# Gated attention and gated FFN on one core: which engine waits for the landings of all transfers at the program's end

## The chip, the cores and the metric

The kernel runs on one core of a Trainium2 chip. The core has five engines with a program each: TensorE (PE in the profile; PEld are its weight loads), VectorE (DVE), ScalarE (ACT), GpSimd (POOL) and SyncE (SP). They meet only through semaphores. Transfers between the chip's memory and the core are issued from an engine's queue and raise a semaphore when they land. The metric is the device time of one execution in microseconds (us); several executions are timed and the median is given.

## The reference

Two branches work on 2048 tokens of width 512, and a gate mixes them. Branch A is a linear-memory attention with 32 heads of width 16 in 4 segments of 512 tokens; branch B is a gated FFN of width 1792. Both read the same x.

```python
g = sigmoid((x * gate_w).sum(-1, keepdims=True))
a = A(x)                                   # attention with memory, then @ wo
b = ((relu(x @ W_gate)) * (x @ W_up)) @ W_down
out = g * a + (1 - g) * b

# A, for each segment s of 512 tokens (q, k, v = x @ wq, x @ wk, x @ wv):
p = softmax(q_s @ k_s.T / 4 + causal_mask)
a_mem = (phi(q_s) @ M) / (phi(q_s) @ z + 1e-6)     # phi(t) = t + 1 if t > 0 else exp(t)
o_s = sigmoid(beta) * a_mem + (1 - sigmoid(beta)) * (p @ v_s)
M, z = M + phi(k_s).T @ v_s, z + phi(k_s).sum()
```

The output is 2048 x 512 in bf16.

## The kernel before

The work is cut into 4 segments of 512 tokens, as the reference has them. For each segment there are projections (q, k, v), attention tiles of scores that ScalarE turns into exponentials and GpSimd masks, products with v, the memory's update and reading, the FFN in 14 slices of 128 columns, and at the end of a segment's work the output product. `outp` (L1056 and after) forms the output of 128 tokens at a time: the products with `wo` (L1074) and with `wd` (L1081) are summed in one PSUM bank, VectorE (L1090) or ScalarE (L1091) scales the bank into a buffer `osb`, and SP issues the store to `out` (L1093). The last tile of 128 tokens is split in columns 0 to 384 and 384 to 512, each with its own scaling and its own store; the store of the last 128 columns, 32 KB, is the last transfer of the program.

The order of all this is not written by hand. `program` describes each operation with its engine or engines, a planned duration and what it reads and writes; a list scheduler (`Sched`) places the operations one after the other on the engines by planned start times, and keeps for every engine a list `prog[engine]` of waits and instructions. `Sched.place` spreads the transfers over 16 semaphores, `dma0` to `dma15`. It takes the one whose last transfer is planned to land first, and has the issuing engine wait for that earlier transfer. `sc.semval` is the value that a semaphore has after a transfer, `sc.cnt` counts the transfers on it, and `sc.dma_end` is the planned landing of its latest one. Almost all transfers are issued from SP's queue; ScalarE issues three small ones at the start.

`Sched.emit` then writes the lists out, engine by engine: an item `("wait", semaphore, value)` becomes a `wait_ge` (L534), and any other item the instruction itself. A wait stands in its engine's program in order: what follows it on that engine starts after it.

After the scheduler has run, the last lines of `program` append waits for the latest transfer of each of the 16 semaphores, in the order of their planned landings, the latest first, so that the program doesn't end before the last transfer has landed. This list is appended to SP's program. Nothing is put on any engine's list behind it.

```python
    sc.run()
    for i in sorted(range(sc.ndma), key=lambda i: -sc.dma_end.get(i, 0.0)):
        if sc.cnt[f"dma{i}"]:
            sc.prog["sp"].append(("wait", f"dma{i}", sc.semval[f"dma{i}", sc.cnt[f"dma{i}"]]))
```

Of the kernel before, what the change touches and what calls it, by code (L numbers as in the profile page):

```python
# [560 lines left out]
def build_kernel(nc, A_x, A_wq, A_wk, A_wv, A_wo, A_beta, W_g, W_u, W_d, gate_w, out):  # L561
    _, S, D = A_x.shape
    F = W_g.shape[1]
    assert D == 512 and S % 512 == 0 and F % 128 == 0
    NSEG, KT, NF, NT = S // 512, D // 128, F // 128, S // 128
    EPS, SCALE = 1e-6, 16 ** -0.5
    sc = Sched(seeds=(237719, 74891, 0, 89398, 0, 53401, 416309, 0, 0, 0, 710933, 0, 718714, 120896, 538430, 820480, 585027, 870794, 793690, 0, 589972, 0, 0, 0, 454998, 16783, 0,))
    T = {}
    with contextlib.ExitStack() as stack:
        for name, shape, dt in plan(S, D, F):  # L570
            T[name] = stack.enter_context(nc.sbuf_tensor(name, shape, dt))
        PS = stack.enter_context(nc.psum_tensor("ps", [128, 8, 512], F32))
        for st in sc.streams:
            sc.sem[st] = stack.enter_context(nc.semaphore(f"s_{st}"))
        program(sc, nc, T, PS, A_x, A_wq, A_wk, A_wv, A_wo, A_beta, W_g, W_u, W_d, gate_w, out, NSEG, KT, NF, NT, EPS, SCALE)
        sc.emit(nc)
    return sc


def program(sc, nc, T, PS, A_x, A_wq, A_wk, A_wv, A_wo, A_beta, W_g, W_u, W_d, gate_w, out, NSEG, KT, NF, NT, EPS, SCALE):  # L580
# [583 lines left out]
    sc.run()  # L1164
    for i in sorted(range(sc.ndma), key=lambda i: -sc.dma_end.get(i, 0.0)):
        if sc.cnt[f"dma{i}"]:
            sc.prog["sp"].append(("wait", f"dma{i}", sc.semval[f"dma{i}", sc.cnt[f"dma{i}"]]))


def bass_gated_mix__memory_aug_infini_attn__glu_gated_reglu__prompt_kernel(  # L1170
# [31 lines left out]
```

## Time and profile before

| what | value |
|---|---|
| median of 3 runs | 263.29 us (262.95 to 263.42) |
| profiled execution's own time | 263.54 us |
| its span, first to last instruction of the program | 262.3 us |
| granted TensorE clock | 1.000 |
| TensorE busy | 255.7 us, 97% of the span |
| ScalarE, VectorE, GpSimd busy | 184.5, 179.5, 130.7 us |
| moved by transfers | 19.87 MB |

The profile is of one execution. Its span goes from the first to the last instruction of the program; the execution's own time is 1.24 us longer than the span. A row of a timeline gives the start in us from the span's start, the length in us, the engine, the line of the kernel, the operation with its tiles, and in brackets how long the engine sat idle before and what ended that. SPq and ACTq are instructions of an engine's sequencer, such as waits and issues of transfers; they are not counted as busy time. An EVENT_SEMAPHORE is a wait that stands as an instruction of its own. The list of issues gives for a transfer the time from its issue to its landing.

### The profile page before, as it was taken

How to read it: one execution, taken by the hardware profiler on the slowest of the kernel's cores; microseconds unless marked ns; L12 is line 12 of the kernel's file. 1: busy time of each engine (PE TensorE's matmuls, PEld its weight loads, DVE VectorE, ACT ScalarE, POOL GpSimd, SP SyncE). 2: the span in 40 equal slices, each digit the busy share in tenths (PEclk: the TensorE clock that was granted, in tenths of full speed). 3: DMA queues.
4: the chain of work that ended last, by engine and by line, in shares of the span. 5: the costliest groups of instructions: out<-in, count | busy, mean ns of one | idle time of the engine just before them, and what ended most of it. 6: DMA issues, size and time to landing. Idle time of an engine off the chain costs nothing.

```text
span 262.3 us, 6420 instructions
## 1 busy us (share of the span) xinstructions
PE 255.7 (97%) x2619; PEld 114.7 (44%) x2653; DVE 179.5 (68%) x356; ACT 184.5 (70%) x160; POOL 130.7 (50%) x295
## 2 busy tenths in 40 slices
PE   8999999999999999999999999999999999999997
PEld 5444443444344544434444544444444444444444
DVE  5488878788986577778788577757667716467600
ACT  4586689999789779785778687677777665576021
POOL 3036557564646457666645457846364454545100
PEclk9999999999999999999999999999999999999999
DMA  6999746930261135212040232010132100100011
GB/s 200 290 308 249 162 63 135 287 46 22 66 143 40 24 74 109 62 23 24 19 107 7 56 96 27 2 41 2 22 82 43 23 21 22 40 2 2 0 42 40
DMA packets 34925, 19.87 MB, mean 76 GB/s; under 512 B 24016, under 2 KB 34128, under 8 KB 34896
## 3 DMA queue, kind: packets, MB, share of 16 engines
q1 hardware_dynamic: 34800, 19.46, 31.6%
q8 instruction: 21, 0.34, 0.6%
q14 instruction: 8, 0.07, 0.1%
q10 hardware_dynamic: 96, 0.00, 0.0%
HBM read 10.40 MB, written 2.11 MB: 48 GB/s over the span
## 4 chain that ended last, share of the span: by engine, by line
PE 97%; issue 1%; DVE 1%
PE ps L1042 38%; PE ps L1081 19%; PE ps L792 11%; PE ps L912 9%; PE ps L968 6%; PE ps L790 5%; PE ps L1074 5%; PE ps L855 1%; PE ps L692 1%; PE ps L706 1%; PE ps L835 0%; DVE hT L1053 0%; DVE Tn L978 0%; DVE osb L745 0%; DVE osb L1090 0%
## 5 line engine op out<-in xcount | busy, mean ns | idle before, releaser
L934 POOL TENSOR_SCALAR_AFFINE_SELECT E<-E 64x256 bf16<-64x256 bf16 (+1 forms) x256 | 110.3, 442 | 112.2 <-ACT E L928 82.9
L928 ACT ACTIVATE E<-ps 128x2048 bf16<-128x2048 f32 x72 | 135.1, 1876 | 38.7 <-PE ps L912 38.6
L1042 PE MATMUL ps<-xT,wu 128*128 128x512 bf16 x213 | 57.2, 380 | 1.4 <-issue 1.3
L1042 PE MATMUL ps<-xT,wg 128*128 128x512 bf16 x219 | 57.7, 380 | 0.6 <-issue 0.3
L1081 PE MATMUL ps<-wd,hT 128*128 128x512 bf16 (+2 forms) x229 | 52.8, 367 | 0.9 <-issue 0.6
L1053 DVE TENSOR_TENSOR hT<-ps,rl 128x512 bf16<-128x512 f32 x56 | 38.5, 687 | 16.6 <-PE ps L1042 16.4
L1081 PEld LDWEIGHTS ps<-wd,hT 128*128 128x128 bf16 x238 | 21.4, 98 | 23.8 <-issue 2.4
L1042 PEld LDWEIGHTS ps<-xT,wg 128*128 128x128 bf16 x224 | 20.6, 98 | 25.7 <-issue 2.8
L1042 PEld LDWEIGHTS ps<-xT,wu 128*128 128x128 bf16 x224 | 20.1, 98 | 25.4 <-issue 3.5
L912 PE MATMUL ps<-qT,kp 32*128 32x192 bf16 (+7 forms) x512 | 28.6, 287 | 0.0
L978 DVE STREAM_TRANSPOSE Tn<-ps 128x512 f32<-128x512 f32 x32 | 21.3, 696 | 8.7 <-PE ps L968 8.7
L1051 DVE TENSOR_SCALAR rl<-ps 128x512 bf16<-128x512 f32 x30 | 20.7, 690 | 8.5 <-PE ps L1042 8.2
L1090 DVE TENSOR_SCALAR osb<-ps,omg 128x512 bf16<-128x512 f32 (+1 forms) x8 | 5.6, 701 | 26.0 <-PE ps L1081 15.1
L1050 ACT ACTIVATE rl<-ps 128x512 bf16<-128x512 f32 x26 | 15.5, 598 | 10.0 <-PE ps L1042 9.7
L912 PEld LDWEIGHTS ps<-qT,kp 32*128 32x128 bf16 x512 | 8.2, 92 | 25.3 <-issue 13.1
L968 PE MATMUL ps<-E,vaug 64*17 64x128 bf16 (+7 forms) x512 | 18.7, 283 | 0.0
L968 PE MATMUL ps<-E,vsh 64*17 64x128 bf16 (+7 forms) x512 | 18.3, 283 | 0.0
L1091 ACT ACTIVATE osb<-ps,omg 128x512 bf16<-128x512 f32 (+1 forms) x9 | 6.1, 674 | 16.4 <-PE ps L1074 14.0
L792 PE MATMUL ps<-xT,wq 128*128 128x512 bf16 x61 | 16.0, 390 | 0.4 <-issue 0.3
L1074 PE MATMUL ps<-wo,oT 128*128 128x512 bf16 (+2 forms) x67 | 16.2, 366 | 0.2 <-issue 0.2
L792 PE MATMUL ps<-xT,wk 128*128 128x512 bf16 x60 | 15.6, 380 | 0.4 <-issue 0.3
L968 PEld LDWEIGHTS ps<-E,vaug 64*17 64x17 bf16 x512 | 11.6, 86 | 8.5 <-issue 4.4
(68 smaller groups left out, 233.6 us busy)
## 6 DMA issues: line engine op xcount, KB each, us to landing
vsh<-vaug SPq DMA_DIRECT2D x8, 272.0 KB, 4.2
osb<-in_A_x_dram SPq DMA_DIRECT2D x16, 128.0 KB, 2.3
out_dram<-osb SPq DMA_DIRECT2D x15, 128.0 KB, 1.7
wg<-in_B_W_gate_dram SPq DMA_DIRECT2D x8, 224.0 KB, 5.7
wu<-in_B_W_up_dram SPq DMA_DIRECT2D x8, 224.0 KB, 6.2
wd<-in_B_W_down_dram SPq DMA_DIRECT2D x1, 1792.0 KB, 10.6
hT<-in_A_x_dram SPq DMA_DIRECT2D x2, 256.0 KB, 2.9
wq<-in_A_wq_dram SPq DMA_DIRECT2D x4, 128.0 KB, 3.5
```

What stands on the lines that cost most here:

```text
L792: ins = e.matmul(A(ep)[:, :], lhsT=w[:, kt, col * 128:(col + 1) * 128], rhs=V.xT[:, kt, tok:tok + 512], start=(kt == 0), stop=(kt == KT - 1))
L912: ins = q.matmul(dst, lhsT=V.kp[r, kslot(s, G), c, :], rhs=V.qT[r, qslot(s, G), q0:q0 + w], start=True, stop=True, tile_position=(32 * jj, ...
L928: acts.append(act(lambda a: a.activation(V.E[:, base * 512:base * 512 + min(2048, 4 * W)], PF[:, 0:min(2048, 4 * W)], ACT.Exp, scale=SCALE ...
L934: pools.append(pool(lambda g, ap=ap, lim=lim, pat=pat: g.affine_select(out=ap, in_=ap, compare_op=ALU.is_ge, fill=0.0, base=lim, pattern=[ ...
L968: ins = q.matmul(A(eps[p])[32 * jj:32 * jj + 17, 64 * (c + u):64 * (c + u + n)], lhsT=v[:, 8 * G + 2 * jj + p, :], rhs=V.E[r, f:f + 64 * n ...
L978: ds.append(dve(lambda e, p=p, ep=eps[p]: e.transpose(V.Tn[:, 2 * (G % (TNN // 2)) + p, :], A(ep)[:, :]), t_dve(512), writes=[f"Tn{2 * (G ...
L1042: ins = e.matmul(A(ep)[:, :], lhsT=w[:, kt, f * 128:(f + 1) * 128], rhs=V.xT[:, kt, c % XR * 512:(c % XR + 1) * 512], start=(kt == 0), sto ...
L1050: evs.append(sc.add(Op([("act", lambda e, ep=eg, r=r: e.activation(V.rl[:, r, :], A(ep)[:, :], ACT.Relu), t_act(512)), ("dve", lambda e, e ...
L1051: ("dve", lambda e, ep=eg, r=r: e.tensor_scalar(V.rl[:, r, :], A(ep)[:, :], 0.0, None, ALU.max), t_dve(512))],
L1053: evs.append(dve(lambda e, ep=eu, r=r, hs=hs: e.tensor_tensor(V.hT[:, hs, :], A(ep)[:, :], V.rl[:, r, :], ALU.mult), t_dve(512), reads=[f" ...
L1074: ins = e.matmul(A(ep)[:, 0:c1 - c0], lhsT=V.oT[:, ot[G], i * 128:(i + 1) * 128], rhs=V.wo[:, G, c0:c1], start=st_ and G == 0, stop=sp_ an ...
L1081: ins = e.matmul(A(ep)[:, 0:c1 - c0], lhsT=V.hT[:, slots[f], i * 128:(i + 1) * 128], rhs=V.wd[:, f, c0:c1], start=st_ and f == f0, stop=sp ...
```

## The change

The 16 waits are appended to ScalarE's program in place of SP's. The list, its order and its values are the same, and so is all that the scheduler placed before it: the loop runs after `sc.run()`. ScalarE's last instruction ahead of the waits is then its last scaling at L1091, and SP's last instruction is the issue of the last store at L1093.

```diff
--- before.py
+++ after.py
@@ -1164,7 +1164,7 @@
     sc.run()
     for i in sorted(range(sc.ndma), key=lambda i: -sc.dma_end.get(i, 0.0)):
         if sc.cnt[f"dma{i}"]:
-            sc.prog["sp"].append(("wait", f"dma{i}", sc.semval[f"dma{i}", sc.cnt[f"dma{i}"]]))
+            sc.prog["act"].append(("wait", f"dma{i}", sc.semval[f"dma{i}", sc.cnt[f"dma{i}"]]))
```

## The prediction

> **What bounds the kernel now.** I read the page first, for the shares and the chain that ended last.
>
> ```profile
> span 262.3 us, 6420 instructions
> PE 255.7 (97%) x2619; PEld 114.7 (44%) x2653; DVE 179.5 (68%) x356; ACT 184.5 (70%) x160; POOL 130.7 (50%) x295
> ...
> PE 97%; issue 1%; DVE 1%
> ```
>
> TensorE is busy 255.7 of 262.3 us, and the chain of work that ended last is 97% matmuls. The edit touches none of that: it is about what happens after the last matmul. So the second view is the end of the timeline, ScalarE, VectorE and the issues of SP's queue together.
>
> ```profile
> 256.52 0.69 ACT L1091 ACTIVATE osb<-ps,omg 128x512 bf16<-128x512 f32 x1 [3.20 <-PE ps L1074]
> ...
> 259.44 0.58 ACT L1091 ACTIVATE osb<-ps,omg 128x384 bf16<-128x384 f32 x1 [2.24 <-PE ps L1074]
> 259.97 0.27 PEld L1074 LDWEIGHTS ps<-wo,oT 128*128 128x128 bf16 x4
> 260.02 0.39 PE L1074 MATMUL ps<-wo,oT 128*128 128x128 bf16 x4
> 260.05 0.33 SPq L1093 DMA_DIRECT2D out_dram<-osb  x1
> 260.45 0.35 DVE L1090 TENSOR_SCALAR osb<-ps,omg 128x128 bf16<-128x128 f32 x1 [10.86 <-PE ps L1074]
> 260.83 0.33 SPq L1093 DMA_DIRECT2D out_dram<-osb  x1
> ```
>
> Columns: start, length, engine and line. The last matmuls end at 260.41, VectorE scales the last 128 columns until 260.80, and SP issues the last store at 260.83 to 261.16. ScalarE has nothing after 259.44 + 0.58 = 260.02. From 260.80 to the end at 262.3 no compute engine works; 1.5 us of the span belong to the last store alone. The third view is the list of DMA issues in the last 2.3 us, with the time from issue to landing in the last column.
>
> ```profile
> out_dram<-osb SPq DMA_DIRECT2D x1, 96.0 KB, 1.6
> out_dram<-osb SPq DMA_DIRECT2D x1, 32.0 KB, 1.5
> ```
>
> The store of 96 KB lands at about 260.05 + 1.6 = 261.65, and that of 32 KB at about 260.83 + 1.5 = 262.33, which is the end of the span to the tenth. The fourth view is the line of the waits themselves, L534, on SP's queue after 261 us (first row), on ScalarE's in the whole span and on ScalarE's after 250 us (the columns are the shortest, median and longest duration in ns, then the first and last start in us).
>
> ```profile
> L534 SPq EVENT_SEMAPHORE  x8: 28/28/567, 261.2 to 261.7; - x8
> ```
>
> ```profile
> L534 ACTq EVENT_SEMAPHORE  x10: 17/17/38, 61.2 to 256.5; - x10
> ```
>
> ```profile
> L534 ACTq EVENT_SEMAPHORE  x2: 17/17/17, 251.8 to 256.5; - x2
> ```
>
> The sixteen waits of the program's end are eight instructions, so two waits stand in each. They start between 261.2 and 261.7, right behind the last issue's end (261.16), in steps of 0.5 / 7 = 0.07 us. One of them is 567 ns long, and it can only be the last: 261.7 + 0.567 = 262.3, the end of the span. **So the built program ends with the wait for the store that lands last**, although the source lists the waits with the latest planned landing first. The other seven are passed in the shadow of the landing.
>
> **The change part by part.**
>
> Taken from SP: eight wait instructions of about 0.07 us each, 8 x 0.07 = 0.56 us on the queue, the time of the last landing not counted. They start at 261.2 and would be through at 261.16 + 0.56 = 261.72 if everything had landed; the landing is at 262.3. They lie in its shadow with 0.6 us to spare, so taking them away gives 0. No DMA issue stands behind them, so no transfer starts earlier either: the 32 KB store waits for VectorE (260.45 + 0.35 = 260.80, issue at 260.83), not for SP.
>
> Given to ScalarE: the same eight. ScalarE's sequencer gets past an ACTIVATE to the next wait when that ACTIVATE starts: its last L534 starts at 256.5, as does the ACTIVATE of 256.52. So the new waits are reached at about 259.44. Each costs what a wait costs here; SP's step of 0.07 us is the nearest row, and ScalarE's own durations of 17 to 38 ns are of the size of SP's 28. Before the 96 KB store (issued 260.05) lands, all pairs without the last two stores pass: six at most, 6 x 0.07 = 0.42 us, done by 259.9. The seventh is held until 261.65 and the eighth until 262.3. Behind these waits ScalarE has no instruction, and nobody waits for ScalarE after its ACTIVATE of 259.44, whose store of 96 KB SP issues on its own at 260.05. ScalarE sees the last landing when SP would have seen it: cost 0, with the difference of their pass times, 28 against 38 ns, as the size of what could be off.
>
> What SP does after its last issue now: nothing. It is through at 261.16 and ScalarE, not SP, is the engine that all others wait for when the program ends.
>
> **The one term that isn't zero** lies behind the span: how the engines tell each other that all have ended. The profiled execution took 263.54 us, its span 262.3, so 1.24 us lie around the span. The trace of before shows no row of the meeting at the end. The nearest rows are those of the opening, the first instruction of each engine after the meeting that precedes the program:
>
> ```profile
> L1187 SPq DRAIN  x1: 7/7/7, 0.0 to 0.0; - x1
> L1187 DVEq DRAIN  x1: 10/10/10, 0.1 to 0.1; - x1
> L1187 ACTq DRAIN  x1: 8/8/8, 0.1 to 0.1; - x1
> ...
> L1187 PEldq DRAIN  x1: 8/8/8, 0.3 to 0.3; - x1
> ```
>
> SP starts first, ScalarE 0.1 and TensorE 0.3 us later: the release runs away from SP, from engine to engine. If the meeting at the end is of that form, SP is its turning point, and with SP as the last to come the release goes straight out. With ScalarE last, its arrival first has to travel to SP and then come back the same way: by these rows 0.1 us more. The bounds: -0.1 us if ScalarE, lying nearer to TensorE than SP does (0.3 - 0.1 = 0.2 against 0.3), may release it directly; +0.3 us if the arrival costs the whole distance that these rows show. I take +0.1, because ScalarE's own row says 0.1.
>
> The Trainium skill has a figure for this meeting ("Runtime: NRT & Kernel Launch", section "The ~15µs preamble/postamble breakdown"): a signal that runs through the five engines and back, some 44 ns a step. If SP stands at one end and ScalarE three steps from it, that rule gives, as an estimate, 3 x 0.044 = 0.13 us in place of my 0.1, and so 263.42 us. The page also gives the closing stages some 5 us in all, and here only 1.24 us stand around the span, so the trace does not bear out its larger figures.
>
> **Sum.** Span: 262.3 + 0 - 0. Around it: 1.24 + 0.1 = 1.34. The profiled execution would take 263.64 for 263.54. That execution is 0.25 us over the median of the three runs (263.29), so the same +0.1 on the median gives **263.4 us**. A difference of 0.2%, 0.53 us, is about what can be told from no change here (the three runs lie between 262.95 and 263.42): under 262.76 is faster and over 263.82 slower.
>
> **Rivals.**
>
> *The source's order holds on ScalarE (slower).* The code lists the latest landing first. If ScalarE's waits are built in that order, the first pair is held until 262.3 and seven are passed behind it, 7 x 0.07 = 0.49 us in the open: 263.29 + 0.49 + 0.1 = 263.88 us, slower. It decides from (0.53 - 0.1) / 7 = 0.061 us a pair. Against it speaks SP's row: the same list came out with the longest wait last, and nothing in the trace says that the build treats ScalarE otherwise. 0.06.
>
> *The time is taken at SP's end (faster).* Then the landing would leave the time: SP would end at 261.16 and not at 262.3, 1.14 us earlier, 262.15 us. Against it: the time of the profiled execution exceeds the span by 1.24 us, room enough for a meeting of all engines behind the last instruction. 0.04.
>
> *The landing hid something that comes out.* Two cases hang here. Eight more instructions on ScalarE could mean one more load of its instructions:
>
> ```profile
> q8 instruction: 21, 0.34, 0.6%
> q14 instruction: 8, 0.07, 0.1%
> ```
>
> q14 has 8 packets in 0.1% of 16 engines' time, so 0.001 x 16 x 262.3 / 8 = 0.5 us each. ScalarE reaches the waits at 259.44 and is needed at 262.3, so 0.5 us has a cover of 2.9 us: 0, and 263.4 stays. Or the new build shifts the matmuls' 255.7 us a little, one way or the other; the runs of one and the same kernel differ by 263.42 - 262.95 = 0.47 us, so I price this at 0.5 us either way, 262.9 to 263.9. Nothing in the profile speaks for it, as no instruction ahead of 261.16 changes its engine or its place. 0.08 for both, of which 0.02 end faster and 0.03 slower.
>
> **How the numbers follow.** The forecast, no measurable change at 263.4 us, has 0.82. Faster: 0.04 + 0.02 = 0.06. Slower: 0.06 + 0.03 = 0.09. Within 0.2%: 0.82 + 0.03 = 0.85. The range starts from the runs' own spread with the bounds of the meeting: 262.95 - 0.1 = 262.85 at the low end, and 263.42 + 0.3 = 263.72 at the high end, which I carry on to 263.9 to take in the first rival (263.88). Outside it stands the time at SP's end and some of the last rival, about 0.08.
>
> **What would show it.** In the profile after, eight L534 instructions on ScalarE's queue should start at about 259.4, two of them long: one ending near 261.7, one, the last, at 262.3, some 0.6 us after the other. SP's queue should end at 261.16 with the last issue, the 32 KB store should be issued at 260.83 and take 1.5 us, and the span should be 262.3. The time beyond the span should grow from 1.24 to about 1.34. I am wrong if the long wait is the first and not the last on ScalarE, if the span ends well after the last landing, if the span ends with SP's issue, or if the stretch ahead of 260.8 changes its length.

## The result, and the profile after

The changed kernel takes 263.87 us (median of 9 runs, 263.19 to 264.08) where the kernel before took 263.29 us beside it (9 runs, 262.76 to 263.56): a ratio of 1.0021, with a 95% interval of 1.0011 to 1.0030. That is 0.55 us more by the ratio, right at the 0.2% that the prediction took as the bound of what can be told. So it is a small loss: the forecast of +0.1 us has its sign and about a fifth of its size, and 263.87 us is 0.05 us beyond the 263.82 from which the prediction called a kernel slower.

Little or none of it is in the program itself. The head of the page after:

```profile
span 262.2 us, 6420 instructions
PE 255.1 (97%) x2619; PEld 113.9 (43%) x2653; DVE 180.1 (69%) x356; ACT 184.5 (70%) x160; POOL 130.6 (50%) x295
```

The number of instructions is the same, the span is 262.2 us for 262.3, and TensorE's busy time is 255.1 us for 255.7. The end of the timeline after, in the order of the prediction's second view (start, length, engine, line):

```profile
259.31 0.58 ACT L1091 ACTIVATE osb<-ps,omg 128x384 bf16<-128x384 f32 x1 [2.24 <-PE ps L1074]
259.84 0.27 PEld L1074 LDWEIGHTS ps<-wo,oT 128*128 128x128 bf16 x4
259.89 0.39 PE L1074 MATMUL ps<-wo,oT 128*128 128x128 bf16 x4
259.92 1.11 SPq L1093 DMA_DIRECT2D out_dram<-osb  x2
260.32 0.35 DVE L1090 TENSOR_SCALAR osb<-ps,omg 128x128 bf16<-128x128 f32 x1 [10.86 <-PE ps L1074]
```

All of it stands 0.13 us earlier than before and in the same distances: the last store is issued by 259.92 + 1.11 = 261.03 (before 261.16). The landings in the list of issues after 260 us:

```profile
out_dram<-osb SPq DMA_DIRECT2D x1, 96.0 KB, 1.6
out_dram<-osb SPq DMA_DIRECT2D x1, 32.0 KB, 1.5
```

And the waits, L534 on ScalarE's queue after 259 us (shortest, median and longest in ns, first and last start in us):

```profile
L534 ACTq EVENT_SEMAPHORE  x8: 38/38/1812, 259.3 to 261.6; - x8
```

Eight instructions, the first as the last ACTIVATE starts, one of them 1.8 us long and the last starting at 261.6. The span ends with it, at 262.2.

What did change stands beside the span. Every run has a time and a span of its own; their difference is very steady, while the spans themselves scatter by 0.9 us (261.5 to 262.4 in the nine runs after). The profiled execution before took 263.54 us with a span of 262.3, so 1.24 us lay around it; the nine runs after have 1.66 to 1.73, median 1.69. The experiments therefore measure this difference, called "around the span" below, beside the ratio.

### The profile page after: what moved, and what is told of

Its sections match the earlier page's. It is cut to its first block, busy times and chain, and to the rows that moved or that the text cites. A ratio compares the mean times of both kernels' runs of the same rounds, so it can differ in the third digit from the quotient of the medians.

```text
span 262.2 us, 6420 instructions
## 1 busy us (share of the span) xinstructions
PE 255.1 (97%) x2619; PEld 113.9 (43%) x2653; DVE 180.1 (69%) x356; ACT 184.5 (70%) x160; POOL 130.6 (50%) x295
## 4 chain that ended last, share of the span: by engine, by line
PE 94%; DMA 3%; issue 2%; SPq 1%; DVE 0%
PE ps L1042 36%; PE ps L1081 19%; PE ps L792 11%; PE ps L912 9%; PE ps L968 6%; PE ps L790 5%; PE ps L1074 5%; DMA xT<-in_A_x_dram 1%; PE ps L855 1%; DMA hT<-in_A_x_dram 1%; SPq L620 1%; PE ps L706 1%; PE ps L835 0%; DVE hT L1053 0%; DVE osb L1090 0%
## 5 line engine op out<-in xcount | busy, mean ns | idle before, releaser
L1091 ACT ACTIVATE osb<-ps,omg 128x512 bf16<-128x512 f32 (+1 forms) x9 | 6.1, 675 | 16.4 <-PE ps L1074 14.0
L790 PE MATMUL ps<-wv,xT 128*128 128x512 bf16 x63 | 15.3, 380 | 0.1
```

The costliest lines, as they stand in the source:

```text
L790: ins = e.matmul(A(ep)[:, :], lhsT=V.xT[:, kt, tok + col * 128:tok + (col + 1) * 128], rhs=w[:, kt, :], start=(kt == 0), stop=(kt == KT - 1))
```

## The experiments

The theory was the prediction's: all engines meet behind the program, the last to come decides, and ScalarE is a dearer place to come last from than SP. It had to explain 0.46 us, not 0.1.

### The kernel before, once more

No edit.

> The kernel before once more, unchanged, so that each of its runs has a span beside its time. If what the change costs lies around the span (1.24 us in the one profiled execution before, 1.66 to 1.73 us in the nine runs after), every run here should stand 1.2 to 1.3 us over its span, and the ratio to the kernel before should be 1.000. If the distance between time and span simply scatters, it should reach 1.7 us in some runs here too, and then the change costs nothing that can be told.

Twelve runs gave 1.18 to 1.27 us around the span (median 1.23), and the 35 runs of the kernel before on that chip 1.19 to 1.30 (median 1.23). The spans went from 261.5 to 263.1 us. The ratio was 1.0004 (0.9991 to 1.0017). So the 0.46 us around the span is a property of the change, and the ratio, with an interval of 0.13% either way, can hardly see it.

### Both engines wait

```diff
-            sc.prog["sp"].append(("wait", ...))
+            for e in ("sp", "act"):
+                sc.prog[e].append(("wait", ...))
```

> All sixteen waits on SP and the same sixteen on ScalarE. Theory 'ScalarE comes last': the end costs what it costs after the change, since ScalarE still comes when the last store has landed: some 1.68 us between time and span, some 0.4 us over the kernel before. Rival 'SP ends too early' (what costs is that SP, with its transfers still under way, has left its program): with SP held until the landing the cost goes, 1.24 us between time and span and the time of the kernel before.

Around the span 1.66 to 1.73 us, median 1.70; ratio 1.0009 (0.9998 to 1.0020). The span ends with both engines: eight waits on each, SP's last 0.566 us long.

```profile
L534 SPq EVENT_SEMAPHORE  x8: 28/28/566, 261.0 to 261.5; - x8
```

Holding SP until the landing gives nothing back. That SP ends early is not what costs; what ScalarE does is. As the later runs show, this experiment could not tell ScalarE's lateness from the mere length of its program, since it has both.

### The list turned round

```diff
-    for i in sorted(range(sc.ndma), key=lambda i: -sc.dma_end.get(i, 0.0)):
+    for i in sorted(range(sc.ndma), key=lambda i: sc.dma_end.get(i, 0.0)):
```

with the waits on ScalarE.

> The waits on ScalarE with the list turned round, so that the wait for the last landing should be built first and seven passes stand behind it. The prediction's first rival priced this at 7 x 0.07 = 0.49 us; by ScalarE's own step in the profile after (259.317 to 259.393, 0.077 us) it is 7 x 0.077 = 0.54 us. Expected: the last wait instruction ends about 0.5 us after the last landing, the span is 0.5 us longer than after the change, and the time is some 0.5 us over that of the changed kernel, about 264.4 us. If the order of the waits makes no difference the time stays at 263.9.

263.78 us, ratio 1.0015 (1.0004 to 1.0027), 1.70 us around the span: as after the change, and not the 264.4 expected. The order of the instructions had not changed, only the two sides in each. The semaphores that each of the eight instructions names in the trace, by their numbers (104 is `dma0`, 112 and 113 belong to the last two stores):

```
after:             105,106  104,108  119,107  118,109  117,110  116,111  115,112  114,113
list turned round: 106,105  108,104  107,119  109,118  110,117  111,116  112,115  113,114
```

The build pairs the list from its middle outwards, so the first and the last item share the last instruction, whichever way round the list is. The durations changed with the sides, though:

```profile
L534 ACTq EVENT_SEMAPHORE  x8: 38/38/38, 259.3 to 262.1; - x8
```

With the late semaphore named first no instruction is long, and the last one starts only at 262.1, when the landing has come. An instruction with two waits starts in the profile when the first is met, and its length holds the second. That is why SP's last row before had 567 ns.

### The waits on GpSimd

```diff
-            sc.prog["sp"].append(("wait", ...))
+            sc.prog["pool"].append(("wait", ...))
```

> The waits on GpSimd in place of ScalarE. If the cost is the way of the late engine's signal to SP and back, and the engines stand in a row TensorE, ScalarE, GpSimd, VectorE, SP, GpSimd is one step nearer than ScalarE: time minus span about 0.04 us less than after the change, so 1.64 us, and the time about 0.4 us over the kernel before. If only SP is a cheap place (or ScalarE alone a dear one), it is 1.68 (or 1.24).

1.73 to 1.84 us around the span, median 1.77, ratio 1.0022 (1.0008 to 1.0035). The order "one step nearer, so a little cheaper" is wrong: GpSimd is dearer than ScalarE. The reason is in the meeting itself, below.

### Eight idle instructions on ScalarE, SP waits as before

```diff
             sc.prog["sp"].append(("wait", f"dma{i}", ...))
+            sc.prog["act"].append(("wait", f"dma{i}", 16))
```

> SP waits as before the change; ScalarE gets sixteen waits too, but for the first landing on each semaphore, long past, so eight more instructions that hold nothing and are through at about 260.0. Theory 'ScalarE comes last': nothing changes, 1.23 us between time and span as before the change. Rival 'ScalarE's program is longer' (what costs is eight more instructions on ScalarE, wherever the end is waited for): a part of the 0.46 us stays. In the traces the meeting of the engines takes 0.14 us more with ScalarE last (262.177 to its release at 262.607 against 262.305 to 262.594); the rest, 0.32 us, is open, so this rival gives 1.23 + 0.32 = 1.55 us.

This splits the cost. The eight instructions on ScalarE hold nothing and are over long before the end, and SP comes last as before:

```profile
L534 ACTq EVENT_SEMAPHORE  x8: 38/38/38, 259.2 to 259.7; - x8
```

Still the runs have 1.52 to 1.60 us around the span, median 1.56, 0.33 more than before. The ratio of the times, 1.0003 (0.9992 to 1.0014), can't show this: 0.33 us would be 0.0013 of the time, inside its interval, and the spans of these ten runs happen to be shorter (median 261.9 us, against 262.0 for the kernel before beside them). Most of the change's 0.46 us has nothing to do with where the landing is waited for.

### One wait on ScalarE, fifteen on SP

```diff
-            sc.prog["sp"].append(("wait", ...))
+            sc.prog["act" if i == 9 else "sp"].append(("wait", ...))
```

> Only the wait for the last store's semaphore moves to ScalarE, the other fifteen stay on SP: ScalarE gets one instruction more and still comes last. Theory 'ScalarE comes last': all of the cost, 1.69 us between time and span. Rival 'ScalarE's program is longer': 1.23 + 0.14 = 1.37 us.

Around the span 1.34 to 1.43 us, median 1.37: the 1.37 of the second reading, to the hundredth. ScalarE is the last to come:

```profile
L534 ACTq EVENT_SEMAPHORE  x1: 17/17/17, 262.1 to 262.1; - x1
```

So coming last from ScalarE costs 0.14 us, and the length of its program the other 0.33: 1.23 + 0.14 + 0.33 = 1.70, where the change has 1.69. The ratio, 1.0016 (1.0006 to 1.0026), is larger than 0.14 us would make it; its spans (median 262.2, against 262.0 for the kernel before beside it) have the rest, with no mechanism that these runs show.

### The waits on VectorE and on TensorE

The same edit with `"dve"` and with `"pe"`.

> The waits on VectorE. If the engines stand in a row TensorE, ScalarE, GpSimd, VectorE, SP and the signal of the late one goes to SP and back, VectorE is the nearest neighbour: about 0.04 us less in the meeting than GpSimd or 0.08 less than ScalarE, 1.61 us between time and span if the open 0.32 us come with every engine but SP, and 1.29 if they come with ScalarE alone.

> The waits on TensorE, the far end of the row: 0.04 us more than ScalarE in the meeting, so 1.73 us between time and span if the open 0.32 us come with every engine but SP, and 1.41 if they come with ScalarE alone. As single waits on TensorE took 51 ns where SP's took 17, some 0.05 us may come on top.

VectorE has 1.35 us around the span (1.31 to 1.37), TensorE 1.52 (1.46 to 1.56), with ratios of 1.0007 (0.9993 to 1.0020) and 1.0013 (1.0000 to 1.0026). Both fall near the reading in which the open part belongs to ScalarE alone (1.29 and 1.41, or 1.46 with the 0.05 for TensorE's slow waits), and far below the other (1.61 and 1.73).

No row of a view shows the meeting, but the trace keeps the updates of the semaphore on which the engines meet. The end of the last wait and the meeting's nine updates, in us from the span's start (updates ahead of the last wait's end belong to engines that had come already):

```
waits on       last wait ends   updates of the meeting's semaphore
SP (before)        262.305      260.588 260.622 260.660 260.951 262.431 | 262.474 262.513 262.547 262.594
VectorE            261.571      259.845 259.879 259.917 261.717 261.740 | 261.837 261.876 261.912 261.958
ScalarE, one       262.162      260.426 262.275 262.314 262.358 262.381 | 262.479 262.518 262.552 262.599
ScalarE (after)    262.177      260.486 262.287 262.325 262.368 262.392 | 262.488 262.527 262.561 262.607
TensorE            262.057      262.243 262.277 262.315 262.358 262.382 | 262.479 262.518 262.553 262.600
GpSimd             262.680      260.950 260.984 263.212 263.256 263.279 | 263.376 263.415 263.451 263.497
```

The engine with the waits is always the one before whose update the row pauses: TensorE first, ScalarE second, GpSimd third, VectorE fourth, SP fifth. Five updates run up the row, in steps of 0.02 to 0.04 us where no engine is waited for, and four run back, in steps of 0.03 to 0.05. The turn at SP takes 0.04 us where SP came last and 0.10 where it had come before. From the last wait's end to the ninth update it takes 0.29 us from SP, 0.39 from VectorE, 0.43 and 0.44 from ScalarE, 0.54 from TensorE, and 0.82 from GpSimd, whose own update comes only 0.53 us after its last wait (ScalarE's after 0.11). Set against what is measured around the span:

| waits on | meeting, us over SP's | around the span, us over 1.23 |
|---|---|---|
| VectorE | 0.10 | 0.12 |
| ScalarE, one instruction | 0.15 | 0.14 |
| TensorE | 0.25 | 0.29 |
| GpSimd | 0.53 | 0.54 |
| ScalarE, eight instructions | 0.14 | 0.46 |
| SP, eight idle ones on ScalarE | 0.00 | 0.33 |

In four rows the meeting explains all, to 0.04 us. Both rows with eight more instructions on ScalarE have 0.32 to 0.33 us that the meeting doesn't show. Eight more on VectorE, TensorE or GpSimd cost nothing of the kind.

### Is it each instruction, or a step?

Idle waits as above, but in four instructions (the eight waits of `dma0` to `dma7`), in sixteen, and eight of them in the middle of ScalarE's program.

```diff
+            if i < 8:
+                sc.prog["act"].append(("wait", f"dma{i}", 16))
```

> As with the eight idle waits on ScalarE, but eight waits in four instructions, SP's waits as before the change. If each instruction more on ScalarE costs the same (0.33 / 8 = 0.04 us), 1.23 + 0.16 = 1.39 us between time and span. If it is a step that some length of ScalarE's program crosses, 1.23 or 1.56 and nothing between. The one instruction more of the run with a single wait on ScalarE showed no cost beyond the meeting's 0.14, which speaks for a step.

```diff
+            sc.prog["act"] += [("wait", f"dma{i}", 16), ("wait", f"dma{i}", 32)]
```

> The same with 32 idle waits in sixteen instructions on ScalarE. A cost per instruction gives 1.23 + 16 x 0.04 = 1.89 us between time and span, a step once crossed stays at 1.56.

```diff
+            sc.prog["act"].insert(200, ("wait", f"dma{i}", 16))
```

> The sixteen idle waits stand in the middle of ScalarE's program (in front of item 200 of its list, some 60% into it) and not at its end, SP's waits as before the change. If the 0.33 us come from the length of ScalarE's program, 1.56 us between time and span again. If they come from waits at the very end of ScalarE's program, 1.23. The span may grow a little, as ScalarE's sequencer spends 8 x 0.077 = 0.6 us there.

Around the span: 1.25 us with four (1.21 to 1.30), 1.26 with sixteen (1.21 to 1.30), 1.57 with eight in the middle (1.50 to 1.59). The ratios are 1.0009 (0.9983 to 1.0036) with four and 1.0017 (1.0007 to 1.0026) with eight in the middle. So it is neither a price per instruction nor a threshold that stays crossed: one, four and sixteen more cost next to nothing around the span, eight cost 0.33 us, and it doesn't matter where in ScalarE's program they stand. It depends on the length of ScalarE's program.

With sixteen a cost shows inside the span. The page of that run counts one load of instructions more on q14 (8 in all the other runs):

```profile
q14 instruction: 9, 0.07, 0.1%
```

and its transfers after 259.5 us show that load beside the last store, which took 2.0 us to land where it took 1.4 or 1.5 in the profiles before and after and in all others of this study:

```profile
q14 instruction: 1, 0.01, 0.9%
issues: line engine op xcount, KB each, median us to landing
out_dram<-osb SPq DMA_DIRECT2D x1, 96.0 KB, 1.6
out_dram<-osb SPq DMA_DIRECT2D x1, 32.0 KB, 2.0
```

The load runs from 260.96 to 261.49 us. Of the last store's sixteen landings fifteen have come by 261.633 us, and the last comes at 262.189. SP's last wait is 1.1 us long there for 0.57 before:

```profile
L534 SPq EVENT_SEMAPHORE  x8: 27/28/1126, 260.6 to 261.1; - x8
```

The spans of its ten runs have a median of 262.6 us, with 261.9 for the kernel before beside it, and the ratio is 1.0022 (1.0004 to 1.0041). Sixteen instructions more thus cost about as much as eight, or more, by another way. ScalarE itself was held there too: it announced its end in the meeting at 260.501 us, 0.52 us after its last wait had ended (259.977), where the changed kernel takes 0.11; SP came later still, so this cost nothing.

The likeliest reading joins the two: ScalarE's instructions come in loads of 8 KB; with sixteen more, a further load falls due while the program still runs and collides with the last store, and with eight more it falls due behind the program, where ScalarE has to wait for it. Of the first half, the load beside the late landing is shown, in one profile, and only the run with sixteen more has it. The second half is argued only.

The traces do show where the 0.33 us is not. Behind the nine updates they have those of a second meeting, the last of them 1.44 us after SP's last wait, in the kernel before (263.745) and with eight idle instructions (263.452) alike. Take from a profiled execution's time the time from the span's start to this last update: -0.18 to -0.21 us are left in the eight profiles in which ScalarE doesn't have exactly eight instructions more, and +0.12 us in all six in which it has. So the cost stands outside this whole stretch, behind the second meeting or ahead of the span. No record there says what it is, and its cause stays open.

### The last landings in the first pair

```diff
-    for i in sorted(range(sc.ndma), key=lambda i: -sc.dma_end.get(i, 0.0)):
+    late = sorted(range(sc.ndma), key=lambda i: -sc.dma_end.get(i, 0.0))
+    for i in late[14::-2] + late[1::2]:
```

with the waits on ScalarE.

> All sixteen waits on ScalarE, in an order that puts the two last landings into the first pair (the pairs are built from the middle of the list outwards, as the rows of the run with the list turned round show). The prediction's first rival at last: the first pair is held until the last landing, seven pairs are passed behind it, 7 x 0.077 = 0.54 us, so the last wait ends 0.54 us later after the landing than after the change; time minus span stays at 1.69, and the time is some 0.5 us over that of the changed kernel. If ScalarE passes them faster than its step, less.

```profile
L534 ACTq EVENT_SEMAPHORE  x8: 38/38/601, 261.3 to 262.4; - x8
```

Four runs. Now the long one is the first (261.3 + 0.6 = 261.9, when the last store lands), and seven follow it to the end of the span at 262.5, 0.56 us after the landing where the changed kernel ends 0.03 after it. Around the span 1.71 us; 264.32 us in all, ratio 1.0039 (1.0024 to 1.0054), so 1.0 us over the kernel before for 0.46 + 0.54 expected. The order of the waits counts, and the kernel before has it right by the way in which the build pairs them.

## Why the prediction was right and wrong

The step on what is **taken from SP** was right: 0. The last store was issued as before, landed in 1.5 us as before, and the stretch ahead of it kept its distances.

The step on what is **given to ScalarE** was right in all that the views of the profile show: eight instructions from the start of the last ACTIVATE, one held until the 96 KB store, the last until the 32 KB store, and the span ending 0.03 us after the landing. The steps are of 0.077 us for the 0.07 assumed.

**The one term that isn't zero** was right in mechanism and near in size. The signal did have to travel up to SP and back; the run with one wait on ScalarE has +0.14 us for the +0.1 that was taken from the rows of the opening. The way up, from ScalarE's update to SP's, takes 262.287 to 262.392 us in the changed kernel, so 0.1 was right for it; the rest is the turn at SP, 0.05 us longer than where SP comes last, less the 0.02 by which ScalarE announces its end sooner after its last wait. The estimate from the Trainium skill's "Runtime: NRT & Kernel Launch" (section "The ~15µs preamble/postamble breakdown"), three steps of 44 ns making 0.13 us, came nearer to the total. The trace agrees with its figure over the whole row, 262.243 to 262.600 us for the eight steps in the run with the waits on TensorE, 0.045 a step, but not for these three steps, which take 0.035 each: that 0.13 is nearer than 0.1 is luck, as what 0.1 lacks is the turn and not longer steps.

What failed is in the third rival: "0.5 us has a cover of 2.9 us: 0, and 263.4 stays". The prediction saw that eight more instructions could mean one more load of ScalarE's instructions, priced the load at 0.5 us, and put it in the only stretch it could see, between 259.44 and the end of the span. The length of ScalarE's program costs 0.33 us outside the span, where this cover doesn't reach, in the runs with eight idle instructions and in the change alike; whether a load is what costs it isn't shown. This term, put at 0, is most of the way from 263.4 to 263.87. The other 0.04 us is the meeting's 0.14 instead of 0.1. What is left of the gap between 263.4 and 263.87, 0.1 us, is inside the scatter of the spans.

That 263.87 lies in the range at all is luck. The spread of the runs and the bounds of the meeting end it at 263.72; it was carried on to 263.9 for the first rival, and what took the time beyond 263.72 was not the first rival but the 0.33 us.

The **first rival** was priced well (0.49 us predicted, 0.54 found with that order forced) and dismissed rightly, by SP's row. Why the build ends with the last landing the prediction did not say: it pairs the list from its middle outwards. The **second rival**, a time that ends with SP, is out: the time grew.

## What to carry to other kernels

The wait that ends a program is best left on the engine at the far end of the row in which the engines meet, which is SP here, with the last landing in the last wait; other places cost 0.1 to 0.5 us. Idle instructions aren't free by being off the path: the length of one engine's program alone moved the time around the span by 0.3 us, up and down again, and in one profile a load came with it beside the last store, which landed half a microsecond later. Where a change moves time that no row of the span shows, subtract the span from the time run by run: ten runs then told 0.1 us apart, while the ratio of the times had an interval of 0.1% or more, 0.3 us, either way.

## What the runs showed of the hardware that was not expected

The length of ScalarE's program: 1, 4, 8 and 16 instructions more gave 0.00, 0.02, 0.33 and 0.03 us around the span (the first after the meeting's 0.14 is taken off), the last with one load of instructions more and a last landing 0.5 us later. The 0.33 us stands outside the stretch from the span's first instruction to the last update of the second meeting, 1.44 us after SP's last wait. GpSimd announces its end 0.53 us after its last wait, ScalarE 0.11, SP 0.13, VectorE 0.15 and TensorE 0.19.
